# Re-dealing the loads and the attention work of batches 1 to 4 in a fused linear-attention and MLP kernel

## The chip, the core and the metric

The kernel runs on one core of a Trainium2 chip. The metric is device time in microseconds (us), median of several runs. The engines are named as the profile names them: PE (matrix unit, with PEld for its weight loads), DVE and ACT (vector and scalar engine), POOL and SP (here mostly issuers of DMA transfers). Each engine works through its own list of instructions in order. The 16 DMA engines are shared by all queues; SP's transfers are one queue (q1 in the page), POOL's another (q0).

## The reference

```python
# q, k, v: (8 batches, 8 heads, 576 positions, 64), float32
def phi(x, c, s):
    r = np.maximum(x, 0.0)
    return np.concatenate([r * c, r * s], axis=-1)     # cos and sin half: 128 features
q_p, k_p = phi(q, cos_w, sin_w), phi(k, cos_w, sin_w)  # angle pi/2 * position / 576
kv  = np.einsum('bhsf,bhsd->bhfd', k_p, v)
z   = np.sum(k_p, axis=2)
num = np.einsum('bhsf,bhfd->bhsd', q_p, kv)
den = np.einsum('bhsf,bhf->bhs', q_p, z)[..., None] + 1e-06
x   = (num / den).transpose(0, 2, 1, 3).reshape(4608, 512)
# MLP: w_in (512, 2048), w_out (2048, 512)
r   = np.maximum(x @ w_in, 0.0)
out = (r * r) @ w_out
```

## The kernel before

A batch has 576 positions: four tiles of 128 (j = 0 to 3) and a tail of 64 (j = 4), the tails of two batches being worked on together in the MLP. For a batch b the attention has these steps, each a function that only issues instructions:

- `load` (L61): q, k or v of a batch, each as one transfer of 1 MB and two small ones for the tail. Every one of q, k, v has two buffers, so batch b+2 takes the buffer of batch b.
- `att_k` (L190): features of k. Per tile a cos half (on DVE with `feat_cos`, or on ACT with `feat_cos_act`) and a sin half (always ACT). `att_v` (L194): v cast to bf16, on DVE or ACT.
- `att_kv` (L222): PE sums k features times v (with a column of ones for z) into the PSUM tile `kz`, and ACT copies it to `kvz`.
- `att_feat` (L254): features of q, cos on DVE and sin on ACT. They are transposed either by PE (`att_t`: `tq`, then copies `qpTp`), in batches 0 and 1, or by a DMA transpose on SP (`att_qT`, L259: `qpT`, two tiles at once, the tail alone), from batch 2 on.
- `att_d` (L617): `num` on PE (L310), then the division `att_div` on DVE (three instructions, L320 to L324) into `x`.
- `x` is transposed by PE (`att_x_pe`, L344: `tx`, then a copy into `xT`) in batches 0 and 1, and by a DMA transpose on SP (`att_x`, L334) from batch 2 on, again two tiles at once.

The MLP runs in numbered slots. `gemm1` (L362) computes a stretch of x times w_in: PE writes `hps`, ACT takes the relu (`rt`, L391), DVE squares (`gT`, L398). `hps` has two buffers, which the PSUM tiles `yh`, `yv`, `yu` of the second product share. `gemm2` (L421) is the product with w_out: for batch 0 in eight parts, for batch 1's first half tile by tile (`tile_mm`), and from then on in pairs of tiles by a seven-product scheme (`pair_mm`, products `ya`, `yv`, `yc`, `yu`) that needs sums of blocks of w_out (`w2_sum`, L494) and of gT (`g_sum`, L510), both on DVE. The slots are:

| slots | work | slots | work |
|---|---|---|---|
| 0-7 | gemm1, batch 0 | 34-41 | gemm1, batch 2 |
| 8-15 | gemm2, batch 0 | 42-49 | gemm2, batch 2 |
| 16-25 | gemm1, batch 1 (24, 25: tails) | 50-59 | gemm1, batch 3 |
| 26-33 | gemm2, batch 1 (30-33: first pair by products) | 60-71 | gemm2, batch 3 |

Nothing is scheduled automatically: `run` (L708) issues a slot's matrix work and then the attention pieces that `at(slot, ...)` put there, in the order in which they were put. In gemm1 slots these pieces come before the square and the block sums; in gemm2 slots the sums come first. `plan` (L625) puts a whole batch: `k` and `f` are the slots of the k/v and the q features of each tile, `kv` the slots of the two parts of `att_kv`, `d` of the divisions, `t` and `x` of the PE transposes. A load, a DMA transpose or a store takes its place in its queue by the same order: SP carries the DMA transposes and the loads from batch 4 on, POOL the loads of batches 1 to 3, all of the weights and, through `put` (L402), the stores. The loads of w_in and of the four blocks of w_out (`load_w2`, 512 KB each as bf16) with those of batches 1 and 2 are issued at the start (L731 to L738).

Of the kernel before, what the change touches and what calls it, by code (L numbers as in the profile page):

```python
# [19 lines left out]
def kernel(  # L20
# [9 lines left out]
    nc = tc.nc  # L30
    P = nc.NUM_PARTITIONS
# [7 lines left out]
    J = S // P  # L39
# [4 lines left out]
    NS = J + 1  # L44
# [16 lines left out]
    def load(src, nm, b, eng):  # L61
        main = inp.tile([P, H, J, D], F32, name=nm, tag=nm, bufs=2)
        tail = inp.tile([P, HH, D], F32, name=nm + "t", tag=nm + "t", bufs=2)
        eng.dma_start(
            out=main[:, :, :, :],
            in_=src[b, :, 0:MAIN, :].rearrange("h (p j) d -> p h j d", j=J),
        )
        for g in range(2):
            eng.dma_start(
                out=tail[g * TAIL : (g + 1) * TAIL, :, :],  # L70
                in_=src[b, g * HH : (g + 1) * HH, MAIN:S, :].rearrange("h p d -> p h d"),
            )
        kqv[nm, b] = (main, tail)

    def load_batch(b, eng, order):
        for nm in order:
            load({"k": k, "v": v, "q": q}[nm], nm, b, eng)
# [12 lines left out]
    def constants():  # L90
        sidx = const.tile([P, J + 1], F32, name="sidx")
        for p0, p1, c, n, base, mult in [
            (0, P, 0, J, 0, J),
            (0, TAIL, J, 1, MAIN, 1),
            (TAIL, P, J, 1, MAIN, 1),
        ]:
            nc.gpsimd.iota(
                sidx[p0:p1, c : c + n],
                pattern=[[1, n]],
                base=base,  # L100
                channel_multiplier=mult,
                allow_small_or_imprecise_dtypes=True,
            )
        bias_pi2 = const.tile([P, 1], F32, name="bias_pi2")
        nc.vector.memset(bias_pi2, math.pi / 2.0)
        theta_scale = (math.pi / 2.0) / S
        nc.scalar.activation(cos_col, sidx, ACTF.Sin, bias=bias_pi2[:], scale=-theta_scale)
        nc.scalar.activation(sin_col, sidx, ACTF.Sin, bias=0.0, scale=theta_scale)
        make_identity(nc, ident)
# [12 lines left out]
    def load_w2(i, n):  # L122
        h0, h1 = i * HB // n, (i + 1) * HB // n
        nc.gpsimd.dma_start(
            out=w2sb[:, h0:h1, :],
            in_=moe_w_out[h0 * P : h1 * P, :].rearrange("(hb p) f -> p hb f", p=P),
        )
# [35 lines left out]
    def xT_of(b, i):  # L163
        return cached(xts, (b, i), [P, KB, 2 * P], "xT", 3)

    def xT_tails(m):

        return cached(xtails, m, [P, 2, 2, 2, TAIL], "xTt", 2)
# [21 lines left out]
    def att_k(b, j, cos=feat_cos):  # L190
        for f in (cos, feat_sin):
            f(kp_of(b, j), piece("k", b, j), j)
# [169 lines left out]
    def gemm1(b, s):  # L362
        if s == 0:
            gTs[b] = mlp.tile([P, HB, MAIN], BF16, name="gT", tag="gT", bufs=1)
        if s == 8:
            gTts[b // 2] = mlp.tile([P, HB, 2 * TAIL], BF16, name="gTt", tag="gTt", bufs=2)
        half = s // 4
        w, nh = (2 * P, 4) if half < 2 else (P, 8)
        h0 = s % 4 * nh
        hps = ps_h.tile([P, nh, w], F32, name="hps", tag="hps", bufs=2)  # L370

        step = P if b == 0 and s % 4 == 0 else w
        for c in range(0, w, step):
            for i in range(nh):
                hb = h0 + i
                for kb in range(KB):
                    out = hps[:, i, c : c + step]
                    if half < 2:
                        rhs = xT_of(b, half)[:, kb, c : c + step]
                    else:  # L380
                        rhs = xT_tails(b // 2)[:, :, kb % 2, kb // 2, :]
                        out = out.rearrange("p (m c) -> p m c", m=2)
                    nc.tensor.matmul(  # L383
                        out=out,
                        lhsT=w1sb[:, kb, hb * P : (hb + 1) * P],
                        rhs=rhs,
                        start=(kb == 0),
                        stop=(kb == KB - 1),
                    )
        rt = mlp.tile([P, nh, w], BF16, name="rt", tag="rt", bufs=2)  # L390
        nc.scalar.activation(out=rt[:, :, :], in_=hps[:, :, :], func=ACTF.Relu)  # L391
        if half < 2:
            dst = gTs[b][:, h0 : h0 + nh, half * w : (half + 1) * w]
        else:
            dst = gTts[b // 2][:, h0 : h0 + nh, :]

        def square():
            nc.vector.tensor_tensor(out=dst, in0=rt[:, :, :], in1=rt[:, :, :], op=ALU.mult)  # L398

        return square  # L400
# [206 lines left out]
    slots, first, second = [], {}, {}  # L607
    for b in range(B):
        n, n2 = 8 + 2 * (b % 2), 4 * len(PAIRS[b]) if b else 8
# [4 lines left out]
    def at(s, fn, *args):  # L614
        after.setdefault(s, []).append((fn, args))
# [6 lines left out]
        att_qT_pe(b, j)  # L622
        att_qT_copy(b, j)

    def plan(b, k, f, kv, d, t=(), x=(), shared=True):  # L625


        for j in range(NS):
            last = j == J or j % 2
            at(k[j], att_k, b, j, feat_cos_act if shared and j % 2 else feat_cos)  # L630
            at(k[j], att_v, b, j, nc.scalar if shared and (b > 2 or j % 2) else nc.vector)
            at(f[j], att_feat, b, j)
            if t:
                at(t[j], att_t, b, j)
            elif last:
                at(f[j], att_qT, b, j // 2)
            at(d[j], att_d, b, j)
            if x:
                at(x[j], att_x_pe, b, j, x[j] > 16)
            elif last:  # L640
                at(d[j], att_x, b, j // 2)
        for i in range(2):
            at(kv[i], att_kv, b, i)


    for j in (2, 3):
# [5 lines left out]
    at(3, att_x_pe, 0, 3, True, nc.vector.tensor_copy)  # L652
    at(12, att_feat, 0, J)
    at(17, att_t, 0, J)
    at(18, att_d, 0, J)
    at(19, att_x_pe, 0, J, True)
    plan(
        1,
        k=(8, 8, 8, 9, 9),
        f=(4, 5, 6, 12, 13),  # L660
        kv=(10, 10),
        d=(11, 13, 15, 17, 19),
        t=(5, 6, 7, 16, 17),
        x=(12, 14, 16, 18, 20),
        shared=False,
    )
    at(14, load_batch, 3, nc.gpsimd, "qkv")
    plan(
        2,
        k=(21, 22, 23, 24, 25),  # L670
        f=(18, 19, 20, 22, 23),
        kv=(26, 26),
        d=(27, 28, 29, 31, 33),
    )
    plan(
        3,
        k=(30, 32, 33, 34, 35),
        f=(27, 29, 31, 32, 33),
        kv=(36, 36),
        d=(37, 38, 39, 40, 41),  # L680
    )
    for b in range(4, B):
        o, p = second[b - 2], first[b - 1]
        at(second[b - 3] + 6, load_batch, b, nc.sync, "kv")
        at(first[b - 2] + 9, load_batch, b, nc.sync, "q")
        plan(
            b,
            k=(o, o, o + 1, o + 1, o + 2),
            f=(o + 4, o + 4, o + 5, o + 5, o + 6),
            kv=(o + 3, o + 4),  # L690
            d=[p + j for j in range(NS)],
        )


    late = {}
    for n, s in ((1, 12), (2, 15)):
        at(s, w2_sum, n)
    for n, s, c in ((4, 18, 0), (4, 19, 1), (3, 30, 0), (3, 31, 1)):
        late.setdefault(s, []).append((w2_sum, (n, c * HB2 // 2, (c + 1) * HB2 // 2)))
    for b in range(1, B):  # L700
        for i, pair in enumerate(PAIRS[b]):
            if (b, i) == (1, 0):
                continue
            for n in range(1, 5):
                s = second[b] + 4 * i - 2 + (0, 1, 1, 2)[n - 1] if i else first[b] + 3 + n
# [13 lines left out]
    with tc.manual_schedule():  # L719
        load_batch(0, nc.sync, "kvq")  # L720
        constants()
        warm(34)
        for j in range(NS):
            att_k(0, j)
        att_v(0, J - 1, nc.gpsimd, H - 1, H)
        att_v(0, 0, nc.vector)
        att_v(0, 1, nc.scalar)
        att_v(0, 2, nc.vector)
        att_v(0, 3, nc.vector, 0, H - 1)
        att_v(0, J, nc.vector)  # L730
        for i in range(4):  # L731
            load_w1(i, 4)
        load_batch(1, nc.gpsimd, "q")
        load_w2(0, 4)
        load_batch(1, nc.gpsimd, "kv")
        for i in range(1, 4):
            load_w2(i, 4)
        load_batch(2, nc.gpsimd, "qkv")  # L738
        att_kv(0, 0)
        att_kv(0, 1)  # L740
        warm(8)
        att_feat(0, 0)
        att_feat(0, 1)
        for j in range(2):
            att_qT_pe(0, j, True)
        for j in range(2):
            att_qT_copy(0, j, True)
            att_num(0, j, True)
        for j in range(2):
            att_div(0, j)  # L750
        att_feat(0, 2, "s")
        att_feat(0, 3, "s")
        for j in range(2):
            fill(4 - j)
            att_x_pe(0, j, True)
        att_feat(0, 2, "c")
        att_feat(0, 3, "c")
        for s in range(len(slots)):
            run(s)
# [29 lines left out]
```

## Time and profile before

| what | value |
|---|---|
| median of 5 runs | 293.9 us (293.53 to 294.29) |
| profiled execution, whole | 292.53 us |
| its span, first to last instruction | 290.8 us |
| granted clock of PE | 1.00 |
| DVE, ACT, POOL busy | 202.0, 164.5, 39.0 us |
| HBM read, written | 36.70 MB, 9.44 MB |
| q1 (SP) packets and bytes | 66816, 29.24 MB |
| q0 (POOL) packets and bytes | 9648, 23.20 MB |

A slot of gemm1 with 256 columns takes PE 1.75 us, a slot of two products of the seven 1.75 us, one `num` 0.25 us, one `att_kv` 1.36 us; the times of slots below come from the starts of PE's matmuls in the timeline of PE. Busy shares are averages over the span; what matters for the change lies between 35 and 125 us.

### The profile page before, as it was taken

Reading aid. Unit: us, or ns where it says so; the run is one execution under the profiler, and the core shown is the slowest. Engines: PE = TensorE matmul, PEld = TensorE weight load, DVE = VectorE, ACT = ScalarE, POOL = GpSimd, SP = SyncE. Lnnn points to the kernel's source line nnn. Section 1 sums busy time; section 2 is a strip of 40 time slices with the busy share of each in tenths; the row PEclk is TensorE's granted clock in tenths of the full one; section 3 lists DMA queues with packets and bytes.
Section 4 is the critical chain, followed back from the end, with each engine's and each line's share of the span. In section 5 each row is a group of like instructions: output and inputs, shape, how many; then the busy total and the mean of one; then the engine's idle time right before and its main releaser. Section 6 shows DMA issues by size and latency. Waiting matters only on the chain.

```text
span 290.8 us, 7285 instructions
## 1 busy us (share of the span) xinstructions
PE 280.1 (96%) x3038; PEld 235.9 (81%) x3045; DVE 202.0 (69%) x450; ACT 164.5 (57%) x251; POOL 39.0 (13%) x67
## 2 busy tenths in 40 slices
PE   8899999998999989999999999999999999999994
PEld 3479855888577979898998888988998888889883
DVE  2467755696399497877598776977677877546584
ACT  3564852679748749555783358835695451265110
POOL 1653405650000000000002000000000000000011
PEclk9999999999999999999999999999999999999999
DMA  7999994999978996799519995399809520300024
GB/s 217 312 204 295 347 236 134 346 359 239 144 137 161 298 199 183 174 280 264 167 73 201 308 208 165 93 257 305 226 0 218 131 46 2 144 2 2 0 78 140
DMA packets 76641, 53.04 MB, mean 182 GB/s; under 512 B 52000, under 2 KB 71712, under 8 KB 76608
## 3 DMA queue, kind: packets, MB, share of 16 engines
q1 hardware_dynamic: 66816, 29.24, 44.3%
q0 software_dynamic: 9648, 23.20, 27.7%
q8 instruction: 24, 0.39, 0.5%
q10 hardware_dynamic: 144, 0.13, 0.1%
q14 instruction: 9, 0.07, 0.1%
HBM read 36.70 MB, written 9.44 MB: 159 GB/s over the span
## 4 chain that ended last, share of the span: by engine, by line
PE 75%; DMA 11%; DVE 6%; ACT 3%; POOL 2%; issue 1%; SPq 1%; DVEq 0%
PE hps L383 35%; PE ya L525 9%; PE yc L525 8%; PE yu L525 7%; DMA q<-in_q_dram 5%; PE yv L525 5%; DMA w2sb<-in_moe_w_out_dram 4%; PE num L310 3%; PE kz L241 3%; DMA v<-in_v_dram 3%; PE yh L432 2%; PE yps L456 2%; PE yps L432 2%; DVE ysb L537 2%; ACT rt L391 1%; DVE u L537 1%
## 5 line engine op out<-in xcount | busy, mean ns | idle before, releaser
L383 PEld LDWEIGHTS <-w1sb 128*128 128x128 bf16 x1312 | 112.9, 98 | 13.7 <-issue 2.9
L383 PE MATMUL hps<-xT,w1sb 128*128 128x256 bf16 (+1 forms) x1056 | 119.1, 269 | 1.1 <-DVE ysb L537 0.6
L391 ACT ACTIVATE rt<-hps 128x1024 bf16<-128x1024 f32 x72 | 73.6, 1023 | 66.8 <-PE hps L383 43.4
L398 DVE TENSOR_TENSOR gT<-rt 128x1024 bf16<-128x1024 bf16 x64 | 44.0, 687 | 21.2 <-ACT rt L391 21.2
L525 PEld LDWEIGHTS <-gs 128*128 128x128 bf16 x480 | 46.9, 98 | 5.4
L525 PEld LDWEIGHTS <-gT 128*128 128x128 bf16 x312 | 29.8, 98 | 3.5
L410 POOL DMA_DIRECT2D out_dram<-ysb x14 | 7.6, 541 | 172.3 <-DVE ysb L537 145.4
L181 ACT ACTIVATE kp<-k,sin_col 128x512 bf16<-128x512 f32 x32 | 22.4, 717 | 2.8 <-DMA k<-in_k_dram 2.8
L324 DVE TENSOR_TENSOR x<-num,rden 128x512 bf16<-128x512 f32 x32 | 22.1, 691 | 1.1
L181 ACT ACTIVATE qp<-q,sin_col 128x512 bf16<-128x512 f32 x32 | 22.1, 721 | 0.7 <-DMA q<-in_q_dram 0.7
L320 DVE TENSOR_SCALAR den<-num 128x8 f32<-128x8 f32 (+1 forms) x40 | 6.6, 164 | 21.3 <-PE num L310 21.3
L521 DVE TENSOR_TENSOR gs<-gT 128x1024 bf16<-128x1024 bf16 x26 | 17.8, 685 | 0.0
L171 DVE TENSOR_SCALAR qp<-q,cos_col 128x512 bf16<-128x512 f32 x32 | 15.1, 499 | 1.7 <-DMA q<-in_q_dram 1.7
L383 PE MATMUL hps<-xTt,w1sb 128*128 128x128 bf16 x256 | 15.1, 219 | 0.8 <-ACT rt L391 0.8
L525 PE MATMUL ya<-w2t,gs 128*128 128x256 bf16 x120 | 15.6, 273 | 0.0
L525 PE MATMUL yu<-w2sb,gs 128*128 128x256 bf16 x120 | 15.5, 273 | 0.0
L525 PE MATMUL yc<-w2sb,gs 128*128 128x256 bf16 x120 | 15.5, 273 | 0.0
L525 PE MATMUL yu<-w2t,gs 128*128 128x256 bf16 x120 | 15.5, 272 | 0.0
L576 ACT COPY s<-yu 128x256 f32<-128x256 f32 x15 | 5.6, 372 | 17.3 <-PE yu L525 17.3
L200 ACT CAST vext<-v 128x512 bf16<-128x512 f32 x23 | 14.1, 614 | 1.0 <-DMA v<-in_v_dram 1.0
L525 PE MATMUL yc<-w2sb,gT 128*128 128x256 bf16 x104 | 13.5, 273 | 0.0
L525 PE MATMUL ya<-w2sb,gT 128*128 128x256 bf16 x104 | 13.5, 273 | 0.0
(93 smaller groups left out, 331.1 us busy)
## 6 DMA issues: line engine op xcount, KB each, us to landing
out_dram<-ysb POOLq DMA_DIRECT2D x14, 512.0 KB, 4.3
k<-in_k_dram SPq DMA_DIRECT2D x5, 1024.0 KB, 7.9
v<-in_v_dram SPq DMA_DIRECT2D x5, 1024.0 KB, 8.6
q<-in_q_dram SPq DMA_DIRECT2D x5, 1024.0 KB, 5.5
q<-in_q_dram POOLq DMA_DIRECT2D x3, 1024.0 KB, 12.6
k<-in_k_dram POOLq DMA_DIRECT2D x3, 1024.0 KB, 9.0
v<-in_v_dram POOLq DMA_DIRECT2D x3, 1024.0 KB, 9.2
w1sb<-in_moe_w_in_dram POOLq DMA_DIRECT2D x4, 512.0 KB, 8.7
```

What stands on the lines that cost most here:

```text
L171: nc.vector.tensor_scalar(out=dst[:, :, 0:D], in0=src, scalar1=0.0, scalar2=cos_col[:, j : j + 1], op0=ALU.max, op1=ALU.mult,)
L181: nc.scalar.activation(out=dst[:, :, D:F], in_=src, func=ACTF.Relu, scale=sin_col[:, j : j + 1])
L200: copy(out=vx[:, j, h0:h1, 0:D], in_=piece("v", b, j)[:, h0:h1, :])
L241: nc.tensor.matmul(out=kz[:, half, hh * E1 : (hh + 1) * E1], lhsT=lhsT, rhs=rhs, start=(j == 0 and hh == 0), stop=(j == J and hh == HH - 1),)
L310: nc.tensor.matmul(out=out, lhsT=lhsT, rhs=kvz[:, half * HH + hh, :], start=True, stop=True)
L324: nc.vector.tensor_tensor(out=x_of(b, j).rearrange("p (b k) (l d) -> p b k l d", b=n, l=2), in0=n4[:, :, :, 0:D].rearrange("p b (k l) d -> ...
L383: nc.tensor.matmul(out=out, lhsT=w1sb[:, kb, hb * P : (hb + 1) * P], rhs=rhs, start=(kb == 0), stop=(kb == KB - 1),)
L391: nc.scalar.activation(out=rt[:, :, :], in_=hps[:, :, :], func=ACTF.Relu)
L398: nc.vector.tensor_tensor(out=dst, in0=rt[:, :, :], in1=rt[:, :, :], op=ALU.mult)
L432: nc.tensor.matmul(out=ypss[b][tt], lhsT=gTs[b][:, hb, tt * P : (tt + 1) * P], rhs=w2sb[:, hb, :], start=(hb == 0), stop=(hb == HB - 1),)
L521: nc.vector.tensor_tensor(out=t[:, :, :], in0=in0, in1=in1, op=op)
L525: nc.tensor.matmul(out=acc, lhsT=lhs[:, hb, :], rhs=rhs[:, hb, :], start=(hb == 0), stop=(hb == HB2 - 1),)
```

## The change

- w_out block 1 (the second of four) is loaded ahead of batch 1's v; the load of batch 3 leaves POOL's queue (slot 14) for SP's (slot 23, order k, v, q); batch 4's k and v stay at slot 32.
- Batch 1: v casts and `att_kv` one slot or more later (10 and 11), its divisions at 12, 14, 16, 17, 20 in place of 11, 13, 15, 17, 19; the division of batch 0's tail at 19 in place of 18. Block sums of w_out 1 and 2 move from slots 12, 15 to 13, 16. The copies of `xT` for odd tiles and the tail go from ACT to DVE.
- Batch 2: all cos halves of k and all v casts but one on DVE; before, ACT had two cos halves and two casts.
- Batch 3: k features at slots 29 to 33 with all four main cos halves on ACT, q features at 33 to 36 (before: 27 to 33), `att_kv` at 37, divisions at 39 to 43 (before: 37 to 41). Batch 4: its main cos halves on ACT. From batch 4 on `att_kv` is one slot later.
- In slots 16 and 20 gemm1 of batch 1 goes 128 columns at a time.

```diff
-        step = P if b == 0 and s % 4 == 0 else w
+        step = P if b < 2 and s in (0, 4) else w
...
-    def plan(b, k, f, kv, d, t=(), x=(), shared=True):
+    def plan(b, k, f, kv, d, t=(), x=(), act_cos=(1, 3), act_v=range(NS), v=None):
...
-            at(k[j], att_k, b, j, feat_cos_act if shared and j % 2 else feat_cos)
-            at(k[j], att_v, b, j, nc.scalar if shared and (b > 2 or j % 2) else nc.vector)
+            at(k[j], att_k, b, j, feat_cos_act if j in act_cos else feat_cos)
+            at((v or k)[j], att_v, b, j, nc.scalar if j in act_v else nc.vector)
...
-                at(x[j], att_x_pe, b, j, x[j] > 16)
+                at(x[j], att_x_pe, b, j, x[j] > 16, nc.vector.tensor_copy if last else nc.scalar.copy)
...
-    at(18, att_d, 0, J)
-    at(19, att_x_pe, 0, J, True)
+    at(19, att_d, 0, J)
+    at(20, att_x_pe, 0, J, True)
     plan(
         1,
         k=(8, 8, 8, 9, 9),
         f=(4, 5, 6, 12, 13),
-        kv=(10, 10),
-        d=(11, 13, 15, 17, 19),
-        t=(5, 6, 7, 16, 17),
-        x=(12, 14, 16, 18, 20),
-        shared=False,
+        v=(10, 10, 10, 10, 10),
+        kv=(11, 11),
+        d=(12, 14, 16, 17, 20),
+        t=(5, 6, 7, 16, 19),
+        x=(13, 15, 17, 18, 21),
+        act_cos=(),
+        act_v=(),
     )
-    at(14, load_batch, 3, nc.gpsimd, "qkv")
     plan(
         2,
         k=(21, 22, 23, 24, 25),
         f=(18, 19, 20, 22, 23),
         kv=(26, 26),
         d=(27, 28, 29, 31, 33),
+        act_cos=(),
+        act_v=(1,),
     )
+    at(23, load_batch, 3, nc.sync, "kvq")
     plan(
         3,
-        k=(30, 32, 33, 34, 35),
-        f=(27, 29, 31, 32, 33),
-        kv=(36, 36),
-        d=(37, 38, 39, 40, 41),
+        k=(29, 30, 31, 32, 33),
+        f=(33, 34, 35, 36, 36),
+        kv=(37, 37),
+        d=(39, 40, 41, 42, 43),
+        act_cos=(0, 1, 2, 3),
     )
     for b in range(4, B):
         o, p = second[b - 2], first[b - 1]
-        at(second[b - 3] + 6, load_batch, b, nc.sync, "kv")
+        at(32 if b == 4 else second[b - 3] + 6, load_batch, b, nc.sync, "kv")
         at(first[b - 2] + 9, load_batch, b, nc.sync, "q")
         plan(
             b,
...
-            kv=(o + 3, o + 4),
+            kv=(o + 4, o + 5),
+            act_cos=(0, 1, 2, 3) if b == 4 else (1, 3),
...
-    for n, s in ((1, 12), (2, 15)):
+    for n, s in ((1, 13), (2, 16)):
         at(s, w2_sum, n)
...
         load_w2(0, 4)
-        load_batch(1, nc.gpsimd, "kv")
-        for i in range(1, 4):
+        load_batch(1, nc.gpsimd, "k")
+        load_w2(1, 4)
+        load_batch(1, nc.gpsimd, "v")
+        for i in range(2, 4):
             load_w2(i, 4)
```

For batch 4 the slot of k and v, 32, is the same number as `second[1] + 6` before.

## The prediction

> **What bounds the kernel.** I read the page first, for the span and the shares.
>
> ```profile
> span 290.8 us, 7285 instructions
> ...
> PE 280.1 (96%) x3038; PEld 235.9 (81%) x3045; DVE 202.0 (69%) x450; ACT 164.5 (57%) x251; POOL 39.0 (13%) x67
> ```
>
> PE is the bound, at a clock of 1.00, and the change adds and removes no matmul work except by splitting. So it can only move PE's waits. The timeline of PE (start, length, instruction, in brackets the idle time and who ended it) shows where they are:
>
> ```profile
> 69.03 1.95 PE L383 MATMUL hps<-xTt,w1sb 128*128 128x128 bf16 x32
> 71.81 1.95 PE L383 MATMUL hps<-xTt,w1sb 128*128 128x128 bf16 x32 [0.84 <-ACT rt L391]
> ...
> 76.79 0.30 PE L241 MATMUL kz<-vextt,kpt 64*128 64x65 bf16 x8 [0.33 <-ACT kpt L181]
> ...
> 90.45 5.40 PE L383 MATMUL hps<-xT,w1sb 128*128 128x256 bf16 x48 [0.63 <-DVE ysb L537]
> ...
> 108.07 0.32 PE L310 MATMUL num<-kvz,qpT 128*64 128x65 bf16 x8 [1.14 <-DVE gs L521]
> ```
>
> Slots 24, 25, 26, 34 and the last `num` of batch 3. From slot 42 on only one wait of 0.26 us per batch is left, so the rest of the span is out of reach. Why slot 25 waits is in ACT's timeline:
>
> ```profile
> 67.48 1.02 ACT L391 ACTIVATE rt<-hps 128x1024 bf16<-128x1024 f32 x1
> 68.40 0.71 ACT L186 ACTIVATE kp<-k,cos_col 128x512 bf16<-128x512 f32 x1
> 69.01 0.71 ACT L181 ACTIVATE kp<-k,sin_col 128x512 bf16<-128x512 f32 x1
> 69.62 0.61 ACT L200 CAST vext<-v 128x512 bf16<-128x512 f32 x1
> 70.13 0.72 ACT L181 ACTIVATE qp<-q,sin_col 128x512 bf16<-128x512 f32 x1
> 70.76 1.00 ACT L391 ACTIVATE rt<-hps 128x1024 bf16<-128x1024 f32 x1
> ```
>
> Between two relus ACT does 2.4 us of features where a slot has 1.75. From start to start a feature costs ACT 0.61, a cast 0.51, a relu 0.92. Last, SP's timeline, for the queue into which the loads move:
>
> ```profile
> 63.59 14.84 SPq L267 DMA_TRANSPOSE qpT<-qp  x2
> 78.53 1.21 SPq L267 DMA_TRANSPOSE qpT<-qpt  x1
> ...
> 93.22 1.77 SPq L64 DMA_DIRECT2D k<-in_k_dram  x1
> 95.09 1.63 SPq L69 DMA_DIRECT2D kt<-in_k_dram  x2
> 96.82 0.55 SPq L64 DMA_DIRECT2D v<-in_v_dram  x1
> 97.47 4.88 SPq L69 DMA_DIRECT2D vt<-in_v_dram  x2
> 102.44 1.22 SPq L342 DMA_TRANSPOSE xTt<-xt  x1
> 103.77 1.20 SPq L267 DMA_TRANSPOSE qpT<-qpt  x1
> ```
>
> This explains the 1.14 at 108.07, which the timeline puts down to a DVE sum: that `num` needs the tail's `qpT`, issued at 103.77 behind the k and v loads of batch 4, landing 4.3 us later, at 108.0. A transpose behind loads lands after them: the loads' last piece landed at 106.5, the `xTt` issued behind it at 107.6.
>
> **Slots 8 to 15.** w_out block 1 lands at 39.65 and holds PE until 39.69: 39.24 to 39.69 is 0.24 over two matmuls' pace. Ahead of v it lands near 36.9, so **+0.24**. v lands 2.8 later (36.85 to about 39.7); its casts on DVE (4 x 0.34 + 0.27 = 1.6) end at 41.3, and `att_kv`, now behind slot 11, starts at 42.9: 1.6 of cover, and without it PE would wait there. One `num` moves out of this stretch into the next, at no cost.
>
> **Slots 16 to 20.** 32 matmuls of 128 columns took 1.79 (18.25 to 20.04 in PE's timeline), 16 of 256 took 1.75: two split slots cost **-0.09**. [...] What the split buys is that slot 16 can start before tile 1's `xT` is copied (0.42 on DVE), now that this division is at slot 14. The new DVE order puts the division of tile 2 (0.19 + 0.24 + 0.60 from start to start = 1.03), two `qpTp` copies (0.68), a block sum (1.13), a square (0.60), a third copy (0.33) and the division of tile 3 (1.03) in a row. From slot 16's end this runs 0.45 to 5.3, while PE reaches tile 3's transposition, behind 1.75 + 1.75 + 1.4 of other work, at 4.9: a new wait of **-0.45** (0 if the sum falls into a hole, -0.8 if DVE's new `xT` copy, 0.34, falls into the row too). DVE is level again by slot 22.
>
> **Slots 21 to 26.** Two cos halves and one cast leave ACT (1.73). Between the relus of slots 22 and 23 stay sin, cast, sin = 1.73, so with the relu 2.65 per 1.75 slot, once: slot 25 waits some 0.27 in place of 0.99 (71.81 - 69.03 - 1.79): **+0.72**. After that ACT is ahead of `kz`: **+0.33**, and 0.1 at `num` 78.86, whose transpose landed at 78.8 among POOL's loads. DVE takes 1.1 more into a stretch in which it idled 0.43 + 0.66 + 1.57 + 1.23 + 1.49.
>
> **Slots 27 to 34.** From DVE go four q-feature halves and one of k (5 x 0.39 = 1.95); its last additions of the pair, at 90.0 before, then follow the product directly. **+0.63**. ACT gets, from slot 29's copy at 83, four groups of 1.73 with two copies of 0.26: done at 92, one relu late by 0.7, which the second `hps` buffer takes. The copies that free `ya` and `yu` end at 85.1 and 87.2; products 6 and 3 write them again at 86.0 and 87.8. All this needs v of batch 3 by 84.3.
>
> So slot 34 could start at 90.45 - (0.24 - 0.09 - 0.45 + 0.72 + 0.33 + 0.1 + 0.63) = **89.0**.
>
> **The SP queue.** Landings here are the trace's records of the transfers. k, v, q of batch 3 (three each) now stand behind the last `qpT` of batch 2, whose tail feature ACT finishes at 72.3; it lands 2.3 later, at 74.6 (2.3 is a transpose with nothing ahead, 228.84 to 231.10). Two loads took 8.2 from the landing of the transpose before them (127.95 to 136.19), so 4.1 each; the three at the start took 11.1 (from 2.4 to 13.5); with 1 MB of stores among them two took 11.5 (159.88 to 171.37), so 0.5 MB of stores costs 1.7. k lands by 79, v by 83 (1.3 of cover, and without it those copies are late and PE waits), q at 86.9, or 88.6 with batch 1's store of 83. Then `xT` of batch 2 (0.9): **89.5** against 89.0: **-0.5** (0 by the 11.1 row; -3.8 by three loads at 11.5 / 2).
>
> SP then stands at the second `xT` until DVE's division at 88.0, and k and v of batch 4 go out at 88.4, 4.8 earlier than before; `xT` lands 90.3, the loads 98.5, with the store of 90 100.2; behind them `xTt` 0.3 and the first `qpT` of batch 3 2.0: 102.5. Its `num`, moved from slot 37 to 39, is due at 89.5 + 6 x 1.75 + 1.36 = 101.3: **-1.2** (-0.4 with loads at 3.7; 0 if the store falls elsewhere; -2.9 with two at 11.5). What is queued on PE behind it waits too; the tail's `qpT`, two transposes later, comes before its `num`, two slots later, so the old wait goes: **+1.14**, and 0.1 at `kz`.
>
> POOL loses nine issues, and batch 0's stores leave at 55 in place of 63.6; nobody waits for them.
>
> **Slots 42 on.** ACT takes two more cos halves of batch 4 in slots 42, 43 (1.2); the copy of `yu` ends 5.0 after slot 42's start and product 3 comes at 5.7. `att_kv` a slot later still leaves three slots before its first `num`. **0**; without the 0.7 of cover PE waits for ACT.
>
> **Sum.** 1.45 up to slot 34, -0.5, -1.2, +1.24: **1.0 us** off 292.53, so 291.5 for the profiled execution, which lay 1.4 below the median; on the median, **292.9**.
>
> **Rivals.** *The loads land in time*: the 11.1 row holds and the stores fall beside the loads. For it: q1 was alone on the engines there. Against it: every k-v pair seen took 8.2 or more. 293.9 - (1.45 + 1.24) = 291.2. *The queue becomes the bound*: five loads in one row on SP with transposes PE waits for behind them. It decides from 2.7 us of waits at slots 34 and 39 together, `qpT` at 103.8 or later without a wait at slot 34. For it: in the trace two `qpT` took 15.2 and 11.1 to land among loads. Against it: POOL's loads, which crowded those, are what moves. All bounds together give 3.8 + 2.9 - 2.7 = 4.0 slower, 297.9; the middle between its threshold and this 295.9. *Nothing measurable*: ACT's and DVE's gains ahead of slot 34 are eaten there, since the chain from 72.3 hardly moves, and the tail's wait only changes place: 293.9.
>
> **Numbers.** Forecast 0.42, in time 0.16, nothing 0.12, queue 0.30. Under 0.2% (0.6 us) a measurement here cannot tell from no change. Faster 0.42 + 0.16 = 0.58, same 0.12, slower 0.30. The range goes from a little below the in-time case, 291.0, to 295.5, short of the queue rival's middle; the forecast's own is 291.7 to 293.3.
>
> **What would show it.** Slot 25 waiting under 0.4; `kz` and slot 34 free of ACT and DVE; a wait at tile 3's `tx` near 59.3; `xT` of batch 2 landing at 89 to 90; the first wait after it at `num` of slot 39 and ended by `qpT`. Wrong would be: waits of ACT's v casts before 84, loads slower than 4.1 each, or ACT missing 5.7 in slots 42 to 45.

## The result and the profile after

| | before | after |
|---|---|---|
| median | 293.66 us (291.97 to 297.70, 47 runs) | 297.26 us (293.74 to 300.32, 28 runs) |
| profiled execution, whole | 292.53 | 298.73 |
| its span | 290.8 | 297.0 |

The changed kernel is slower: ratio 1.0084, interval 1.0063 to 1.0104. The ratio sets the most disturbed runs of both kernels aside and therefore says less (2.5 us) than the two medians (3.6). The forecast was 292.9 with a range up to 295.5; it was wrong. By the granted clock the changed kernel's runs fall in two groups: 16 of the 28 had a mean of 0.987 to 0.994, with a median of 298.3 us, and 12 had 0.997 or more, with 295.7. The profiled execution is of the first group, so the two spans differ by more (6.2) than the medians.

First the page after: span, shares, and the granted clock in 40 slices.

```profile
span 297.0 us, 7342 instructions
...
PE 282.0 (95%) x3070; PEld 236.8 (80%) x3077; DVE 202.1 (68%) x452; ACT 164.1 (55%) x249; POOL 32.6 (11%) x58
...
PEclk9999999999999979999999999999999999999999
```

PE is busy 1.9 us longer than before, though the change gave it no more to compute, and one slice, the fifteenth (104 to 111 us), has a clock below full. Where the rest went is in PE's timeline (start, length, instruction, in brackets the idle time and who ended it). In this execution everything lies 0.8 us later than in that of before from batch 0's first `kz` on (11.33 against 10.53; batch 0's v, a load that the change doesn't touch, landed later). "Over pace" below is the distance between two starts less the time that the matmuls between them take elsewhere.

```profile
60.04 0.40 PE L351 MATMUL tx<-ident,x 128*128 128x128 bf16 x4 [0.36 <-DVE x L324]
...
72.38 1.95 PE L383 MATMUL hps<-xTt,w1sb 128*128 128x128 bf16 x32 [0.23 <-ACT rt L391]
...
91.24 7.16 PE L383 MATMUL hps<-xT,w1sb 128*128 128x256 bf16 x64 [1.36 <-DMA xT<-x]
...
105.95 0.41 PE L310 MATMUL num<-kvz,qpT 128*128 128x65 bf16 x8 [2.74 <-DMA qpT<-qp]
106.20 3.33 PE L383 MATMUL hps<-xT,w1sb 128*128 128x256 bf16 x16
...
109.78 1.97 PE L383 MATMUL hps<-xT,w1sb 128*128 128x256 bf16 x16
...
126.22 1.03 PE L525 MATMUL yc<-w2sb,gs 128*128 128x256 bf16 x8 [1.73 <-DVE ysb L537]
```

Up to 89 us the change did what was forecast: slot 25 waits 0.23 in place of 0.84, the waits at `kz` and for DVE at slot 34 are gone, and tile 3's `tx` has a new wait of 0.36. Then come three new waits: slot 34 for a transpose (1.36), batch 3's first `num` in slot 39 for a transpose (2.74), and slot 48 for a DVE addition (1.73). And a fourth loss stands between two lines that show no wait: the 16 matmuls behind the wait of slot 39 took 3.33, the next 16 took 1.97. By windows (length; busy time of PE, PEld, DVE, ACT, POOL; then the granted clock, the DMA share and GB/s) that is the clock:

```profile
100.00:106.00 6.00, 3.26 (x32) 2.68 (x30) 1.65 (x3) 2.29 (x3) 0.00 (x0) 1.00 1.23 202
106.00:109.50 3.50, 3.50 (x27) 2.58 (x28) 2.26 (x5) 0.00 (x0) 0.00 (x0) 0.57 0.63 140
```

PE stood idle for nearly half of the first stretch and was granted 0.57 of the clock in the next. From 106.20 to 109.78 lie 16 matmuls and a `num`: 3.58 us, where 1.75 and 0.25 are their pace, so 1.6 us are lost behind the wait, on top of it.

The queue behind the first two waits is SP's timeline:

```profile
79.92 0.60 SPq L64 DMA_DIRECT2D q<-in_q_dram  x1
80.56 3.54 SPq L69 DMA_DIRECT2D qt<-in_q_dram  x2
84.22 5.93 SPq L342 DMA_TRANSPOSE xT<-x  x2
90.25 0.53 SPq L64 DMA_DIRECT2D k<-in_k_dram  x1
...
92.35 1.09 SPq L64 DMA_DIRECT2D v<-in_v_dram  x1
...
100.12 5.57 SPq L267 DMA_TRANSPOSE qpT<-qp  x2
105.80 1.22 SPq L267 DMA_TRANSPOSE qpT<-qpt  x1
...
118.26 0.58 SPq L64 DMA_DIRECT2D q<-in_q_dram  x1
```

By the trace's records of the landings, batch 3's last q piece landed at 89.01 and `xT` of batch 2, behind it, at 91.19; k of batch 4 was issued at 90.25, the last piece of its v landed at 104.04, and `qpT`, behind it, at 105.90. The third wait begins at the last line: q of batch 4, issued at 110.95 before, goes out only at 118.26 and lands at 124.92. DVE's timeline shows what that does:

```profile
121.77 0.68 DVE L521 TENSOR_TENSOR gs<-gT,gs 128x1024 bf16<-128x1024 bf16 x1
124.95 0.88 DVE L171 TENSOR_SCALAR qp<-q,cos_col 128x512 bf16<-128x512 f32 x2 [2.49 <-DMA q<-in_q_dram]
125.74 0.42 DVE L537 TENSOR_TENSOR ysb<-yc,s 128x256 f32<-128x256 f32 x1
```

DVE stands 2.49 us at a feature of q, and behind it in its list is the addition that frees the PSUM tile for PE's next `yc`, which PE starts at 126.22. So PE, in the product of batch 2, waits for a load of batch 4, through a queue and an engine that both work in order.

### The profile page after: what moved, and what is told of

Same layout as the page of the kernel before. It is cut to its first block, busy times and chain, and to the rows that moved or that the text cites. A ratio compares the mean times of both kernels' runs of the same rounds, so it can differ in the third digit from the quotient of the medians.

```text
span 297.0 us, 7342 instructions
## 1 busy us (share of the span) xinstructions
PE 282.0 (95%) x3070; PEld 236.8 (80%) x3077; DVE 202.1 (68%) x452; ACT 164.1 (55%) x249; POOL 32.6 (11%) x58
## 4 chain that ended last, share of the span: by engine, by line
PE 79%; DMA 9%; DVE 5%; SPq 2%; issue 1%; ACT 1%; DVEq 0%; ACTq 0%
PE hps L383 40%; PE ya L525 8%; PE yc L525 7%; PE yu L525 6%; DMA q<-in_q_dram 5%; PE yv L525 4%; PE num L310 3%; PE kz L241 2%; DMA xT<-x 2%; PE yps L456 2%; PE yps L432 2%; PE yh L432 2%; DMA qpT<-qp 2%; DVE ysb L537 1%; SPq L69 1%
## 5 line engine op out<-in xcount | busy, mean ns | idle before, releaser
L383 PEld LDWEIGHTS <-w1sb 128*128 128x128 bf16 x1344 | 114.1, 98 | 14.4 <-issue 1.8
L383 PE MATMUL hps<-xT,w1sb 128*128 128x256 bf16 (+1 forms) x1088 | 120.4, 268 | 1.9 <-DMA xT<-x 1.4
L310 PEld LDWEIGHTS <-qpT 128*128 128x128 bf16 (+1 forms) x240 | 10.4, 101 | 5.8 <-DMA qpT<-qp 3.2
L310 PE MATMUL num<-kvz,qpT 128*128 128x65 bf16 (+1 forms) x240 | 11.9, 196 | 2.8 <-DMA qpT<-qp 2.7
L200 ACT CAST vext<-v 128x512 bf16<-128x512 f32 x22 | 13.5, 615 | 1.7 <-DMA v<-in_v_dram 1.7
## 6 DMA issues: line engine op xcount, KB each, us to landing
q<-in_q_dram POOLq DMA_DIRECT2D x2, 1024.0 KB, 13.3
```

The costliest lines, as they stand in the source:

```text
L200: copy(out=vx[:, j, h0:h1, 0:D], in_=piece("v", b, j)[:, h0:h1, :])
L310: nc.tensor.matmul(out=out, lhsT=lhsT, rhs=kvz[:, half * HH + hh, :], start=True, stop=True)
L383: nc.tensor.matmul(out=out, lhsT=w1sb[:, kb, hb * P : (hb + 1) * P], rhs=rhs, start=(kb == 0), stop=(kb == KB - 1),)
```

## The experiments

Three transfers are suspects, one for each wait, and each was put elsewhere alone.

**Batch 3 back on POOL** (`e1_pool_load`).

```diff
-    at(23, load_batch, 3, nc.sync, "kvq")
+    at(14, load_batch, 3, nc.gpsimd, "qkv")
```

> The changed kernel with batch 3's load back on POOL's queue at slot 14, everything else kept. Theory Q (the loads on SP make the DMA transposes behind them late): the wait of slot 34 for xT (1.36 us idle in the changed kernel's profile) goes, since only transposes stand ahead of it; the wait of slot 39 for qpT (2.74) falls to about 1 to 1.5, since batch 4's k and v can go out some 2 us earlier than in the changed kernel; the wait of slot 48 behind batch 4's q (1.73) stays. Sum 2.5 to 3 us below the changed kernel. Rival D (the re-dealt features and divisions overload DVE or ACT, the queue is not the cause): nothing changes at slots 34 and 39, the time stays within 0.5 us of the changed kernel.

297.04 us (295.02 to 298.37, 6 runs), ratio 1.0106, interval 1.0052 to 1.0161. PE's timeline:

```profile
104.38 0.62 PE L310 MATMUL num<-kvz,qpT 128*128 128x65 bf16 x8 [2.90 <-DMA qpT<-qp]
...
124.22 1.03 PE L525 MATMUL yc<-w2sb,gs 128*128 128x256 bf16 x8 [1.39 <-DVE ysb L537]
```

The wait of slot 34 is gone, as expected, but slot 39's didn't shrink: k went out 1.1 earlier (89.15), v's last piece landed at 102.45, `qpT` at 104.33, and PE, no longer held at slot 34, came earlier too. What one wait gave the next took, and the 2.5 to 3 us didn't come. The expectation failed in two steps: k went out 1.1 earlier and not 2, since the second `xT` ahead of it has to wait for DVE's division, and it didn't count that a PE which no longer waits at slot 34 comes to slot 39 earlier too (by 1.7 here, where `qpT` landed 1.6 earlier).

**k and v of batch 4 behind the transposes** (`e2_kv4_behind`).

```diff
-        at(32 if b == 4 else second[b - 3] + 6, load_batch, b, nc.sync, "kv")
+        at(37 if b == 4 else second[b - 3] + 6, load_batch, b, nc.sync, "kv")
```

> The changed kernel with batch 4's k and v issued at slot 37 in place of 32, so behind the qpT transposes of batch 3 on SP. Theory Q: slot 34 still waits about 1.4 us for xT, slot 39 does not wait (qpT lands near 98 against 103), PE's clock stays at 1.00 behind it: 2.7 us of wait and up to 1.7 us of slow matmuls less, so 3 to 4.4 us below the changed kernel, unless ACT now waits for batch 4's v in slot 42 (under 1 us). Rival D: slot 39 still waits, now put down to DVE or ACT; no gain over 0.5 us.

294.67 us (293.33 to 300.01, 12 runs), 1.0023, 0.9993 to 1.0052: 2.6 less than the changed kernel on the medians, 1.8 by the two ratios, by moving one pair of loads five slots later; both are less than the 3 to 4.4 expected. The wait of slot 39 is gone and the clock stays at 1.00; the two others stay (PE's timeline):

```profile
91.92 7.16 PE L383 MATMUL hps<-xT,w1sb 128*128 128x256 bf16 x64 [1.30 <-DMA xT<-x]
...
122.96 1.03 PE L525 MATMUL yc<-w2sb,gs 128*128 128x256 bf16 x8 [1.81 <-DVE ysb L537]
```

**q of batch 4 ahead of batch 3's `xT`** (`e3_q4_early`).

```diff
-        at(first[b - 2] + 9, load_batch, b, nc.sync, "q")
+        at(38 if b == 4 else first[b - 2] + 9, load_batch, b, nc.sync, "q")
```

> The changed kernel with batch 4's q issued at slot 38 in place of 43, so ahead of the xT transposes of batch 3 on SP. Theory L (the later divisions hold back the load of q behind their transposes, the features in slot 46 wait for it, and the additions queued behind these on DVE hold PE in slot 48): q lands by 116, DVE does not wait, the 1.73 us of slot 48 go, 1.7 us below the changed kernel. Rival: DVE's additions are late from the re-dealt work itself, and slot 48 still waits over 1 us.

295.19 us (294.01 to 297.25, 12 runs), 1.0047, 1.0012 to 1.0082: 2.1 less on the medians, 1.1 by the ratios. q went out at 107.70 and landed at 114.44, and slot 48 waits no more; slots 34 and 39 do (the first line names DVE, but `xT` landed at 91.17, just ahead of it):

```profile
91.22 7.16 PE L383 MATMUL hps<-xT,w1sb 128*128 128x256 bf16 x64 [0.95 <-DVE ysb L537]
...
106.60 0.42 PE L310 MATMUL num<-kvz,qpT 128*128 128x65 bf16 x8 [3.42 <-DMA qpT<-qp]
```

**Is the clock's drop made by the wait?** Matmuls of zeros (`fill`, 128x512 each, into a PSUM tile that nobody reads) in the place of the idle time should keep the clock up. In the trace of before eight matmuls of that size took 1.73 us from start to start (79.11 to 80.84), 0.216 each, so 12 are 2.6 us and 7 are 1.5. The first two attempts fill the changed kernel: 12 ahead of the `num` of slot 39 (`e4_fill`), and 7 more ahead of slot 34 (`e5_fill_both`).

```diff
+    at(33, fill, 7)      # e5_fill_both alone
...
+    at(39, fill, 12)
```

> The changed kernel with 12 matmuls of 512 columns on zeros (12 x 0.213 = 2.6 us, results not used) ahead of the first num of slot 39, where PE otherwise idles 2.74 us. Theory C (the idle stretch is what drops PE's clock, 0.57 in the 3.5 us behind it): with PE kept busy in the same wait the clock stays 1.00 in every run and the slow matmuls go: 1.5 to 1.7 us below the changed kernel's profiled execution, and the spread of its runs (293.7 to 300.3) shrinks. Rival: the clock drops for another reason, and the runs stay spread, the median within 0.5 us of the changed kernel's.

> The changed kernel with 7 matmuls on zeros (1.5 us) ahead of the last num of slot 33 and 12 (2.6 us) ahead of the first num of slot 39, results not used, so that PE has work in both waits for a transpose. Theory C (an idle stretch drops the clock): the clock is 1.00 behind both places and near 1.00 in every run, where the changed kernel's runs have 0.987 to 1.0; the median lies 1 to 1.5 us below the changed kernel's 297.3, though the waits themselves stay. Rival: clocks of 0.99 still come, without an idle stretch ahead of them.

Neither told anything about slot 39: 297.57 us (296.69 to 302.22, 6 runs), 1.0115, 1.0069 to 1.0161, and 299.34 (296.90 to 301.96, 6 runs), 1.0181, 1.0131 to 1.0231. In both profiles the loads were later and slot 34 took the wait; PE's timelines of `e4_fill` and then `e5_fill_both`:

```profile
94.06 9.73 PE L383 MATMUL hps<-xT,w1sb 128*128 128x256 bf16 x64 [3.98 <-DMA xT<-x]
```

```profile
93.42 8.73 PE L383 MATMUL hps<-xT,w1sb 128*128 128x256 bf16 x64 [2.04 <-DMA xT<-x]
```

When PE came to slot 39 the transpose had landed, and filling cost time in full; five of `e4_fill`'s six runs kept a clock of 0.998 or more and were no faster for it. But both show the drop at another place: the 64 matmuls behind the wait took 9.73 and 8.73, against 7.16 in the lines above, behind idle times of 3.98 and 2.04; the granted clock between 94 and 100 us was 0.55 and 0.78. They also show that the wait of slot 34 isn't one number: the first `xT` landed at 91.19, 93.38 and 94.01 in three executions of kernels that issue the same transfers up to there.

So the clock was tried again where only one wait is left. `f1_three` has the three moves of `e1` to `e3` at once, and `f3_three_sum` also puts a block sum of w_out back to slot 15. `g1_kv4_ahead` is `f3_three_sum` with k and v of batch 4 at slot 32 again, so that only the wait of slot 39 comes back, and `g2_kv4_ahead_fill` fills that one.

```diff
 # g2_kv4_ahead_fill against g1_kv4_ahead
+    at(39, fill, 12)
```

> The fastest kernel so far (batch 3's load on POOL, batch 4's k, v at slot 37 and q at 38, the second w_out sum at slot 15) with one thing put back: batch 4's k and v at slot 32, ahead of batch 3's qpT on SP. Theory Q: slot 39 waits 2.5 to 3.2 us for qpT, nothing else changes; with the slow matmuls behind it (theory C, half clock for up to 3.4 us) 3 to 4.5 us above that kernel, 294.5 to 296. Rival: the other wait, of slot 34, was what counted, and this one is taken up by slack: under 1 us.

> The kernel of the run before with 12 matmuls on zeros (2.6 us, results not used) ahead of the first num of slot 39, so that PE works through the wait for qpT, in a kernel in which no other long wait comes ahead of it. Theory C (an idle stretch of PE is what drops its clock): the same wait, no slow matmuls behind it, clock 1.00 in slots 39 to 42, 1 to 1.7 us below the run without the filling. Rival: the clock drops all the same, or did not drop without the filling: no gain, or up to 0.3 us of loss.

`g1_kv4_ahead` took 295.53 us (292.80 to 296.60, 12 runs), 1.0018, 0.9983 to 1.0053; `g2_kv4_ahead_fill` 294.10 (293.43 to 295.07, 12 runs), 1.0003, 0.9979 to 1.0026. The windows around the wait, of `g1_kv4_ahead`:

```profile
100.00:104.00 4.00, 2.31 (x22) 1.83 (x19) 1.29 (x2) 2.05 (x2) 0.00 (x0) 1.00 1.33 171
104.00:108.00 4.00, 2.89 (x20) 2.21 (x21) 2.16 (x5) 0.00 (x0) 0.00 (x0) 0.61 0.97 210
```

and of `g2_kv4_ahead_fill`:

```profile
100.00:104.00 4.00, 3.95 (x26) 2.38 (x25) 1.29 (x2) 1.96 (x2) 0.00 (x0) 1.00 1.28 179
104.00:108.00 4.00, 3.50 (x43) 3.01 (x43) 2.69 (x8) 1.02 (x1) 0.00 (x0) 1.00 0.93 196
```

The clock falls to 0.61 in the one and stays at 1.00 in the other, although `qpT` lands as late (105.07 and 104.67). Of `g1_kv4_ahead`'s 12 runs, eight had a mean clock of 0.988 to 0.992 over the whole run and took 294.5 to 296.6 us, four had 0.997 or more and took 292.8 to 294.1; all 12 of `g2_kv4_ahead_fill` had 0.996 or more. That the idle time brings the clock down, and that work of no use prevents it, is therefore shown for this wait, by eight runs of 12 against none. What it is worth is less certain: 1.4 us on the medians, 0.8 on the means, with intervals that overlap. The filling has a price too: the four runs whose clock stayed up without it have a median of 293.3, 0.8 below the filled kernel's. The whole of the one step, wait and clock, is the difference of `g1_kv4_ahead` to `f3_three_sum` (below), a pair of loads five slots earlier: 295.53 to 291.47, 4.1 us on medians that were not taken side by side, 2.5 by the ratios to the kernel before.

**The three moves together, and what the re-deal itself is worth** (`f1_three`, and `f2_two` without the move of batch 3).

> The changed kernel with all three loads moved: batch 3 on POOL at slot 14, batch 4's k and v at slot 37, its q at slot 38. Theory Q with L (order in SP's queue is the whole cause, the re-deal itself gains): no wait over 0.5 us on PE between slots 25 and 50, clock 1.00 throughout, 2.0 to 3.0 us below the kernel before, ratio 0.990 to 0.993. Rival D: the re-deal costs more than it gains elsewhere, ratio 1.00 or above.

> The same with batch 3's load left on SP at slot 23 as in the changed kernel. Theory Q: only the wait of slot 34 for xT (1.4 us) is left, so some 1.5 us slower than with all three moved, ratio to before 0.995 to 0.999; if that wait grows past 3 us in a run, the clock drops there too. Rival: slot 34 would have waited anyway for DVE's additions (0.63 before), then the two differ by under 0.8 us.

`f1_three`: 292.10 us (291.65 to 293.18, 12 runs), 0.9947, 0.9927 to 0.9967. `f2_two`: 292.70 (291.96 to 295.37, 12 runs), 0.9979, 0.9952 to 1.0006. In PE's timeline of `f2_two` only one wait of those above is left, in `f1_three` none over 0.21 between 84 and 130:

```profile
91.67 7.16 PE L383 MATMUL hps<-xT,w1sb 128*128 128x256 bf16 x64 [0.67 <-DMA xT<-x]
```

`f2_two` is 0.6 slower than `f1_three` on the medians and 0.9 by the ratios, not the 1.5 expected: the wait of slot 34 was 0.67 there, where the changed kernel's profile had 1.36. On the medians that is the size which the rival named (under 0.8), but not for its reason: with batch 3 on POOL slot 34 doesn't wait at all, so DVE's additions don't hold it.

So of the changed kernel's 297.26 us 5.2 hung on where three loads stand in a queue, 4.0 by the ratios, and the rest of the change is a gain.

**The new wait of tile 3's `tx`.** `f3_three_sum` undoes one more step.

```diff
-    for n, s in ((1, 13), (2, 16)):
+    for n, s in ((1, 13), (2, 15)):
```

> All three loads moved, and the second sum of w_out blocks back from slot 16 to slot 15. If that sum, standing in DVE's row ahead of batch 1's fourth division, makes the wait at tile 3's transposition in slot 18 (0.36 idle, 0.53 over the pace, in the changed kernel), the wait goes: 0.4 to 0.5 us below the version with the sum at 16. Rival: the wait is the division's own place, slot 17 right behind slot 16's, and stays over 0.3.

291.47 us (291.37 to 292.18, 8 runs), 0.9933, 0.9907 to 0.9958: 0.6 less than `f1_three`, and the `tx` comes without a wait. The block sum of 1.13 on DVE was the one piece too many in the row.

**Three trims** (`f4_trim`, on top of `f3_three_sum`).

```diff
-        step = P if b < 2 and s in (0, 4) else w
+        step = P if b < 2 and s in (0, 4) and (b, s) != (1, 4) else w
...
-        act_v=(1,),
+        act_v=(),
...
-            act_cos=(0, 1, 2, 3) if b == 4 else (1, 3),
```

> The fastest kernel so far with three small things more: batch 2's last v cast from ACT to DVE (0.51 us less between the relus of slots 22 and 23; slot 25 waited 0.4 over the pace), batch 4's cos halves on ACT for odd tiles only, as before the change (product 3 waited 0.2 for ACT's copy), and slot 20 of gemm1 at 256 columns again (0.05). If these are what the profile says, 0.4 to 0.6 us less, 290.9 to 291.1; if DVE is short instead, the waits at num in slots 41 to 43 (0.25 to 0.37) grow and nothing is won.

290.90 us (290.42 to 291.35, 6 runs), 0.9886, 0.9852 to 0.9920, the fastest kernel of the study. The wait of slot 25 is gone, as was expected of the cast that left ACT; what each trim is worth in time was not separated. The cos trim didn't do what it was for; PE's timeline:

```profile
112.43 1.03 PE L525 MATMUL yu<-w2sb,gs 128*128 128x256 bf16 x8 [0.76 <-ACT s L576]
```

A copy on ACT (at 112.02) still stands behind features and a cast of v of batch 4, whose load, now behind the transposes, lands late enough to leave ACT idle for 2.42 us first (to 109.75). Fewer cos halves didn't help an engine that starts late.

**The kernel before, with the one move that mattered most** (`g3_before_kv4`).

```diff
-        at(second[b - 3] + 6, load_batch, b, nc.sync, "kv")
+        at(33 if b == 4 else second[b - 3] + 6, load_batch, b, nc.sync, "kv")
```

> The kernel before with one move: batch 4's k and v issued at slot 33, behind the last qpT of batch 3, in place of 32, ahead of it. Theory Q: the wait of 1.14 us for that qpT at 108.07 goes and nothing else changes: 0.9 to 1.2 us below the kernel before, ratio 0.996 to 0.997. Rival: DVE, to which the timeline puts that wait down, holds PE there anyway; no change.

292.24 us (291.10 to 298.49, 12 runs), 0.9924, 0.9897 to 0.9950. The wait of 1.14 for the tail's `qpT` is gone, its other waits are not (72.70 at slot 25, 91.22 at slot 34). The gain on the medians, 1.8, is more than the wait; seven of the 29 runs of the kernel before beside it had a clock of 0.991 to 0.994 and took 295.7 to 298.5; of the 12 here one had 0.988. That explains little of it: the runs with 0.996 or more have medians of 293.8 and 292.2, still 1.6 apart. What the other 0.5 are stays open, and so does what lowers the clock of the kernel before, whose profile has no idle time over 1.14 from batch 0's first `kz` on.

## Why the prediction was wrong

- **Slots 8 to 26: right.** The w_out block's wait is gone (+0.24; from 39.24 to 39.69 that is over one matmul's pace, not two). Two split slots cost nothing worth seeing: the 32 matmuls of 128 columns took 1.79 (52.85 to 54.64 in PE's timeline) and 1.78 (62.60 to 64.38), 16 of 256 took 1.75 (55.33 to 57.08). The wait at `tx` is 0.53 over pace for 0.45 forecast, slot 25's 0.39 for 0.27, `kz` waits no more.
- **Slot 34 at 89.0 if nothing but PE's own row held it: right.** PE was free at 91.24 - 1.36 = 89.88, less the late start of 0.8, 89.1.
- **Batch 3's loads on SP, -0.5: right mechanism, a third of the size.** The loads kept their forecast: the last piece of q landed at 89.01, less the late start 88.2, for 88.6. The term that was too small is the transpose behind them, 0.9: `xT` landed 2.2 later. The wait is 1.4 over pace, inside the bound of 3.8.
- **Batch 4's k and v ahead of `qpT`, -1.2: right mechanism, less than half of the size.** The term that failed is the time of the two loads. The forecast gave them 8.2, and a 0.5 MB store 1.7, together 9.9; from the landing of the `xT` ahead of them (92.12) to that of v's last piece they took 11.9, in `e1_pool_load` 11.5. That landing was a poor mark to count from: in the row that gave the 8.2, k had been issued 3.3 before it (124.68), here 1.9. Counted from the issue of k, the same pair took 13.3 in the kernel before (93.22 to 106.48, with a 0.5 MB store beside it) and 13.8 here; 13.3 from the forecast's own 88.4 would have made the wait 2.7. It is 2.9 over pace, the size of the bound, whose row had twice the stores: that this fits is luck.
- **The old wait of the tail, +1.14: right.**
- **"Slots 42 on ... 0": this step failed.** It followed ACT's row and `att_kv`, where PE indeed doesn't wait, and forgot what the prediction itself asks of a moved step: the transposes it issues. Batch 3's last divisions went from slots 40 and 41 to 42 and 43, the issues of `xT` with them, and in SP's order q of batch 4 stands behind those. It cost 1.9 over pace in slot 48; `e3_q4_early`, in which that wait goes when q alone moves, shows the cause.
- **The clock: in no step.** 1.6 in the profiled execution. Both queue terms took PE to go on at its pace afterwards. Without it the forecast is wrong all the same: the 12 runs with 0.997 or more have a median of 295.7.

From before to after the spans differ by 6.2, 0.8 of it the late start. The steps as measured give 5.4: -1.4 up to slot 34 and -1.24 at the tail, then +1.4, +2.9, +1.6, +1.9 and some 0.2 in small waits.

Of the rivals, *the queue becomes the bound* was right: the waits of slots 34 and 39 together were 4.3, above its threshold of 2.7. Its price of 295.9, with 297.9 by all bounds, was made from those waits alone; the measured 297.26 lies beyond its middle because of two losses that it didn't hold, the clock and slot 48, 3.5 us together. In hindsight it deserved to lead: the kernel before had a row for this very pair with a store beside it, and for both queue terms the slow bound lay farther off (by 3.3 and 1.7) than the fast one (0.5 and 1.2).

## What to carry to other kernels

A transfer that somebody will wait for soon goes ahead of a prefetch in an in-order queue: five slots' difference for one pair of loads was worth 1.8 us here by the ratios and 2.6 on the medians, and one slot's 1.8 on the medians in the kernel before. When a step is moved, follow every issue that it carries along, then what stands behind those in the queue, then what stands behind the engine instruction that consumes it. And a wait on PE may cost more than itself: each of the six of 2.04 to 3.98 us here had a lowered clock behind it, and in the changed kernel, with 0.50 for 3.41 us behind the 2.74, that was 1.6 us on top; price the matmuls that follow a wait.

## What the hardware showed

- **The clock after an idle stretch.** In the profiled executions each idle time of 2.04 to 3.98 us at slots 34 and 39 was followed by a lowered clock: 2.04 by 0.78 (94 to 100 us of `e5_fill_both`), 2.74 by 0.57 (the changed kernel, above), 2.80 by 0.61 (`g1_kv4_ahead`, above), 2.90 by 0.61 (104.3 to 108 of `e1_pool_load`), 3.42 by 0.72 (106 to 110 of `e3_q4_early`) and 3.98 by 0.55 (94 to 100 of `e4_fill`). After the 1.73 of slot 48, and the 1.81 of `e2_kv4_behind`, the windows show 1.00. These figures are means: the clock's own records in the changed kernel's trace have 1.00 up to 106.50, 0.50 from there to 109.91, which is 3.41 us and begins 0.55 after PE's start at 105.95, and 1.00 again behind. For the others the length is an estimate, from the share that their windows lost, at 0.50 throughout: 3.4 to 3.5 us in four executions, and in `e4_fill` (0.88 in 88 to 94, 0.55 in 94 to 100) 6.8, twice that. What decides it was not shown: no wait at these slots lay between 1.81 and 2.04 in a profile, and `g1_kv4_ahead`, with a drop behind its wait in the profile, kept a mean clock of 0.997 or more in four of its 12 runs.
- **Loads beside stores and transposes.** From the landing of the transpose ahead of them, two loads with a 0.5 MB store took 11.5 and 11.9 us in `e1_pool_load` and the changed kernel, but 9.1 in `e4_fill`, where k had been issued 4.9 ahead of that landing; from the issue of k they took 13.3, 13.8 and 14.0. With no store in flight, behind the transposes (`e2_kv4_behind`, `f1_three`, `f2_two`), they took 10.4 to 11.3 from the issue. In 100 to 106 us of the changed kernel the DMA share was 1.23 at only 202 GB/s. All of that is SP's queue, 3675 of 3968 packets under 512 bytes, so in the main pieces of tails and transposes; those of 256 bytes took 71 ns on the mean between 101 and 102 us, and 18 between 104 and 105. What held them there stays open.
- **A transpose's place behind loads.** `xT` landed 2.2 and `qpT` 1.9 us after the last piece of the loads ahead of them. It isn't one number: 0.9 in `e2_kv4_behind` and 3.7 in `e5_fill_both` for the same `xT`. SP stands in the instruction meanwhile: the first `qpT` of batch 3 took SP 3.75 us to issue (100.12 to 103.87) behind loads, where the tail's took 1.22. In the traces of before and after (84 and 93 transfers on SP) none landed ahead of one issued in front of it: `xTt` at 107.64 behind loads at 106.48 before, `qpT` at 105.90 behind 104.04 after. What holds SP in the instruction was not tried by itself.
